# Six stacked cross layers on one core: a new order for all three engines in the steady unit, and one multiply done in two halves

## Chip, cores, metric

One core of a Trainium2 chip runs the whole program. The metric is device time in microseconds (us), as the median of a kernel's runs. Engines: PE does the matmuls, ACT empties PSUM, DVE does the elementwise work in SBUF.

## The reference

```python
B, F, D, L = 16384, 100, 16, 6
Din = min(F * D, 1024)                       # 1024
x = x0                                       # [16384, 1024] bf16
for l in range(6):
    proj = jnp.einsum('bd,de->be', x, ws[l]) + bs[l]
    x = x0 * proj + x
```

## The kernel before

Batch rows come in 16 pairs of 2 x 512. A **unit** is one pair in one layer, so there are 96 units. A unit computes `x W` by a Strassen-like scheme: seven block products P1 to P7, of which 5 and 2 are split once more into seven half-size inner products (`5p1` to `5p7`, `2p1` to `2p7`). The six units of the first pair and the last unit use a single level. The other 89 are the **steady units** that this text is about.

Names: `P6.0` is product 6, output column block 0 (four matmuls of 512 columns). `5p3` is an inner product (four matmuls of 256 columns). ACT: `E…` adds the bias while emptying a bank, `F.m`, `5f1`, `2f2` … copy one PSUM bank into another so that the next product can add to it, `5e_…` and `2e_…` empty inner results. DVE: `T1` to `T4` and `5t…`, `2t…` are the sums that feed products; `Q1, Ua, Va` finish blocks; `Qm, Um, Vm, Wm` multiply a block by x0; `Qa, Ux, Vx, Wx` add the old x, which completes the next unit's input. W is block 21.

```python
# cut: a rank per operation; one list for every steady unit (SPAN2 = 23.4 apart)
R2 = ranks("""
P1.0@0 5p1@.9 5p5@1.3 P1.1@1.7 P1.2@2.6 5p2@3.5 5p6@3.9 2p1@4.3 2p5@4.8 P1.3@5.2 5p3@6.1 5p7@6.5 2p2@7 2p6@7.4
5p4@8 P6.1@8.5 2p7@9.4 P6.0@9.8 ...
... E4.0@22.1 E4.3@22.7 E4.2@23.2 E4.1@23.8
T1@-1.1 5t13@.2 5t2@2.1 ... Va@21.4 Wm@24.6 Wx@26 Vm@27.9 Vx@29.4
""")
...
        for m in range(KH):      # the last product, and its evictions into W
            group(f"P4.{m}", "4", pA[m], A[m], T[4], ["T4", A[m]], m, False)
            biased(f"E4.{m}", W[:, m, :], pA[m][:], 1, m, [A[m]], [f"W.{m}"])
...
        for nm, C, q in (("Q", Q, (0, 0)), ("U", U, (0, 1)), ("V", V, (1, 1)), ("W", W, (1, 0))):
            ttop(nm + "m", C[:], C[:], blk(x0T, *q), MULT, allm(nm) + [X0[q]], allm(nm))
...
    # cut: operations are emitted greedily by rank once those they depend on are emitted
    heap = [(ops[i][0], i) for i in range(len(ops)) if need[i] == 0]
```

The ranks fix the order of the instructions on each engine. DVE and ACT then run their lists strictly in order (the Trainium skill says so, "Perfetto Trace Analysis", section Tensor Engine Instruction).

Of the kernel before, what the change touches and what calls it, by code (L numbers as in the profile page):

```python
# [10 lines left out]
MULT = mybir.AluOpType.mult  # L11
# [5 lines left out]
def ranks(text):  # L17

    return {w.split("@")[0]: float(w.split("@")[1]) for w in text.split()}
# [3 lines left out]


R2 = ranks("""
P1.0@0 5p1@.9 5p5@1.3 P1.1@1.7 P1.2@2.6 5p2@3.5 5p6@3.9 2p1@4.3 2p5@4.8 P1.3@5.2 5p3@6.1 5p7@6.5 2p2@7 2p6@7.4
5p4@8 P6.1@8.5 2p7@9.4 P6.0@9.8 P3.1@10.7 2p3@11.5 2p4@12 P3.0@12.4 P6.3@13.3 P6.2@14.1 P3.3@15 P3.2@15.9
P7.3@16.7 P7.0@17.6 P7.2@18.4 P7.1@19.3 P4.3@20.2 P4.0@21 P4.2@21.9 P4.1@22.8
5e_p5@2 5f1@2.6 E1.1@3.1 E1.2@3.7 5e_c11@4.2 E1.0@4.7 5f2@5.3 2e_p5@5.7 2f1@6.4 5e_c12@6.8 5e_u3@7.3 2e_c11@7.8
2f2@8.4 E1.3@8.9 F.1@9.6 5e_c21@10 2e_u3@10.5 F.0@11 2e_c12@12.2 E3.1@12.7 2e_c21@13.2 E3.0@13.7 F.3@14.3  # L30
F.2@15.2 E3.3@16.1 E3.2@16.9 E7.3@17.8 E7.2@19.5 E7.0@20.1 E7.1@20.7 E4.0@22.1 E4.3@22.7 E4.2@23.2 E4.1@23.8
T1@-1.1 5t13@.2 5t2@2.1 2t13@3.7 5t4@5.4 2t2@6.9 T2@7.2 T4@8.5 T3@9.6 2t4@10.8 5cc@11.1 2cc@12.8 Q1@13.9 Qm@15.1
Qa@16.4 Ua@17.6 Um@18.9 Ux@20.2 Va@21.4 Wm@24.6 Wx@26 Vm@27.9 Vx@29.4
""")
R0 = ranks("""
P1.0@0 P1.1@.9 P1.2@1.7 P1.3@2.6 P2.2@3.5 P2.3@4.4 P2.1@5.2 P2.0@6.1 P5.2@6.9 P5.1@7.8 P5.0@8.7 P5.3@9.5
# [2 lines left out]
F1.2@2.8 F1.0@3.2 F1.3@3.7 F1.1@4.1 E2.2@4.6 E2.1@6.3 E2.0@7.2 E2.3@7.7 E5.2@8.3 F.2@11.5 E5.1@11.9 E5.3@12.4  # L39
F.1@13.2 E5.0@13.6 E7.2@14.9 E3.2@15.8 F.0@16.4 E7.1@16.8 F.3@17.4 E3.1@17.8 E7.0@19.2 E3.0@19.8 E3.3@20.4  # L40
E7.3@21 E4.0@21.8 E4.2@22.7 E4.1@23.6 E4.3@24.4
Qm@14.5 Qa@18.6 Ua@21.1 Um@22.4 Va@23.5 Wm@25.2 Wx@26.4 Ux@27.6 T1@4.6 Vm@30 Vx@31.2 T2@8.3 T3@9.8 T4@13
c5@-8.6 c6@-6.8 c7@-4.5 c3@11.9 2i7@-7.4 2i5@-7.1 2i6@.5 2i3@9.4 5i5@10.9 5i7@11.2 5i6@11.6 5i3@14.2
""")
RFIRST = {**R0, **ranks("""
# [6 lines left out]
def kernel(  # L52
# [18 lines left out]
    KQ, HQ, NQ = KH // 2, H // 2, NB // 2  # L71
# [20 lines left out]
    P1s, P5s, Q, U, V, W = (work.tile([P, KH, NB], BF16, name=f"ev{i}") for i in range(6))  # L92
# [6 lines left out]
    def blk(t, dh, n):  # L99
        return t[:, n, dh * KH:(dh + 1) * KH, :]  # L100

    def tt(o, a, b, op):
        nc.vector.tensor_tensor(out=o, in0=a, in1=b, op=op)  # L103
# [60 lines left out]
    def op(rank, fn, rd=(), wr=(), weights=()):  # L164
        for k in weights:
            uses_left[k] = uses_left.get(k, 0) + 1
        ops.append((rank, fn, tuple(rd), tuple(wr), tuple(weights)))
# [3 lines left out]
    for u, (pr, l) in enumerate(units):  # L171
        one, first, last = level1(u), u == 0, u == NU - 1
        rk = RFIRST if first else (R0 if one else R2)
        x0T, xst = x0Ts[pr % 2], xsts[pr % 2]
        xs = x0T if l == 0 else xst
        X0 = {q: f"x0.{pr % 2}.{q[0]}{q[1]}" for q in QD}
# [3 lines left out]
        def add(name, fn, rd=(), wr=(), weights=(), rk=rk, base=base, u=u):  # L180
            op(base + rk[name], fn, rd, wr, [(u, w) for w in weights])

        def ttop(name, o, a, b, o_, rd, wr, **kw):
            add(name, lambda: tt(o, a, b, o_), rd, wr, **kw)
# [64 lines left out]
        if not one:  # L249
            for X, Bm, src in (("5", T[1][:], "T1"), ("2", B21, XI[1, 0])):  # L250
                q = lambda dh, n, Bm=Bm: Bm[:, dh * KQ:(dh + 1) * KQ, n * NQ:(n + 1) * NQ]
# [15 lines left out]
        if not one:  # L267
            for X, Bm, src, a, b, C in (("5", T[1][:], "T1", 0, 1, P5s), ("2", B21, XI[1, 0], 2, 3, Q)):
                q = lambda dh, n, Bm=Bm: Bm[:, dh * KQ:(dh + 1) * KQ, n * NQ:(n + 1) * NQ]
# [49 lines left out]
        allm = lambda s: [f"{s}.{m}" for m in range(KH)]  # L319
# [2 lines left out]
        ttop("Ua", U[:], U[:], P5s[:], ADD, allm("U") + allm("5c"), allm("U"))  # L322
        ttop("Va", V[:], V[:], P5s[:], ADD, allm("V") + allm("5c"), allm("V"))
        for nm, C, q in (("Q", Q, (0, 0)), ("U", U, (0, 1)), ("V", V, (1, 1)), ("W", W, (1, 0))):
            ttop(nm + "m", C[:], C[:], blk(x0T, *q), MULT, allm(nm) + [X0[q]], allm(nm))
            if not last:
                ttop(nm + ("a" if nm == "Q" else "x"), blk(xst, *q), C[:], blk(xs, *q), ADD, allm(nm) + [XI[q]], [XO[q]])
            else:
                xfin = xsts[1 - pr % 2][:].rearrange("r n k (j p) -> r (n k j) p", p=P).rearrange(
                    "r (e n j k) p -> r e n j k p", e=2, n=2, j=KH)  # L330
                xo = x0Ts[1 - pr % 2][:].rearrange("r n k (j p) -> r (n k j) p", p=P).rearrange(
                    "r (e n j k) p -> r e n j k p", e=2, n=2, j=KH)
                XF = [f"xs.{1 - pr % 2}.{a}{b}" for a, b in QD]
                XT = [f"x0.{1 - pr % 2}.{a}{b}" for a, b in QD]
                eh, n = q

                def fin(eh=eh, n=n, C=C, xfin=xfin, xs=xs):
                    v4 = lambda a: a.rearrange("r k (j p) -> r k j p", p=P)
                    tt(xfin[:, eh, n].rearrange("r j k p -> r k j p"), v4(C[:]), v4(blk(xs, eh, n)), ADD)
                add(nm + ("a" if nm == "Q" else "x"), fin, allm(nm) + [XI[q]] + XF, [f"xf{eh}{n}"])  # L340

                def tr(eh=eh, n=n, xfin=xfin, xo=xo):
                    nc.sync.dma_start_transpose(out=xo[:, eh, n].rearrange("p j k r -> p (j k) r"),
                                                in_=xfin[:, eh, n].rearrange("r j k p -> r (j k p)"))
                z = base + {"Q": 40, "U": 41, "V": 42, "W": 43}[nm]
                op(z, tr, [f"xf{eh}{n}"] + XT, [f"xt{eh}{n}"])

                def st(eh=eh, n=n, xo=xo, pr=pr):
                    r0 = pr * PR + n * NB
                    nc.sync.dma_start(out[r0:r0 + NB, eh * H:(eh + 1) * H].rearrange("(j p) d -> p j d", p=P),  # L350
                                      xo[:, eh, n].rearrange("p j k r -> p j (k r)"))
                op(z + 10, st, [f"xt{eh}{n}"], ["out"])
# [110 lines left out]
```

## Time and profile before

| | before |
|---|---|
| time, median of 3 runs | 2318.92 us (2318.32 to 2319.11) |
| PE / DVE / ACT busy | 98% / 91% / 79% |
| a steady unit, start to start | 23.63 us, in layer 1 (counted from 0) 23.68; the 88 after the first average 23.65 |
| the same at the pitch of undelayed groups (20 of 0.863 us, 14 of 0.437) | 23.38 us |

From the page of the kernel before: the span, the busy times, and the first line of the chain that ended last.

```profile
span 2316.6 us, 34627 instructions
...
PE 2272.3 (98%) x12674; PEld 1261.3 (54%) x12912; DVE 2102.9 (91%) x2218; ACT 1837.5 (79%) x3223; POOL 20.4 (1%) x41
...
PE 95%; DVE 2%; issue 1%; DMA 1%; SPq 0%; ACT 0%; DVEq 0%; ACTq 0%
```

PE is the bound, but "98% busy" hides the question. The ends of matmuls are modelled, so small gaps vanish in it (a group of four is drawn 1.03 us long below and repeats every 0.86), and one has to read **start to start**. Here is one steady unit, from the timeline of PE of the kernel before. The columns are start in us, length in us, engine, line, operation, out<-in, shapes, count; neighbours that look alike are merged. This trace misses some matmul records (12674 of 12912 are there), so a group of four can show as x3.

```profile
1088.91 1.03 PE L189 MATMUL pA<-xst,wp 128*128 128x512 bf16 x4
1089.77 0.60 PE L287 MATMUL pX<-T,wp 128*128 128x256 bf16 x4
...
1095.42 0.60 PE L287 MATMUL pX<-ti,wp 128*128 128x256 bf16 x4
1095.98 0.60 PE L287 MATMUL pX<-xst,wp 128*128 128x256 bf16 x4
1096.41 1.16 PE L287 MATMUL pX<-ti,wp 128*128 128x256 bf16 x8
1097.41 1.03 PE L189 MATMUL pA<-T,wp 128*128 128x512 bf16 x4
...
1105.63 7.07 PE L189 MATMUL pA<-T,wp 128*128 128x512 bf16 x32
1112.54 1.03 PE L189 MATMUL pA<-xst,wp 128*128 128x512 bf16 x3
```

P1.0 and the group after it start 0.86 us apart; 2p2 and 2p6 (1095.98, 1096.41) 0.43 us. P7 and P4 at 1105.63 take 6.91 us for 32 matmuls, 216 ns each. Against that, 5p7 at 1095.42 is followed by 2p2 after 0.56 us, 0.12 too many. 2p6 and 5p4 (x8 at 1096.41) take 1.00 us where two groups need 0.87, another 0.13 (0.12 in the unrounded starts). From 1088.91 to 1112.54 it is 23.63 us.

ACT at that place, in the kernel before:

```profile
1095.36 0.57 ACT L194 COPY pX<-pX 128x512 f32<-128x512 f32 x1
1095.84 1.08 ACT L194 CAST iu<-pX 128x512 bf16<-128x512 f32 x2
```

The copy is 2f1. It ends at 1095.93, and 2p2, which adds to that bank, starts at 1095.98. The second of the two casts, 5e_u3, empties the bank that 5p4 needs: it ends at 1095.84 + 1.08 = 1096.92, and 5p4 starts 0.44 us before P6.1, at 1096.97. So ACT holds both. DVE in the same unit (T1, 5t13, Wm, 5t2, Wx, 2t13, and after the cut T2 with T4):

```profile
1087.81 1.22 DVE L103 TENSOR_TENSOR T<-xst 128x2048 bf16<-128x2048 bf16 x1
1089.13 0.69 DVE L103 TENSOR_TENSOR ti<-T 128x1024 bf16<-128x1024 bf16 x1
1089.84 1.22 DVE L103 TENSOR_TENSOR ev<-ev,x0T 128x2048 bf16<-128x2048 bf16 x1
1090.98 0.42 DVE L103 TENSOR_TENSOR ti<-T,ti 128x512 bf16<-128x512 bf16 x1
1091.31 1.22 DVE L103 TENSOR_TENSOR xst<-ev,xst 128x2048 bf16<-128x2048 bf16 x1
1092.57 0.69 DVE L103 TENSOR_TENSOR ti<-xst 128x1024 bf16<-128x1024 bf16 x1
...
1096.12 2.54 DVE L103 TENSOR_TENSOR T<-xst,T 128x2048 bf16<-128x2048 bf16 x2
```

T1 to 5t13, which reads what T1 just wrote, is 1.32 us; Wm to 5t2, which are independent, is 1.14. T2 ends at 1096.12 + 1.22 = 1097.34, and P6.1, its first reader, starts at 1097.41. DVE is therefore **just in time** as well.

The duration of 1.22 us is the one that the Trainium skill gives for this operation ("VectorE: DVE Perf Modes", the perf-mode tier table: 1224 ns for a bf16 tensor_tensor of 2048 columns).

### The profile page before, as it was taken

The numbers are of one execution on the slowest core, as the hardware profiler recorded it, in microseconds if no ns is written. First come the engines' busy times: TensorE is split into PE (matmuls) and PEld (weight loads), VectorE is DVE, ScalarE is ACT, GpSimd is POOL, SyncE is SP. The second block draws the span as 40 slices with busy tenths as digits, with TensorE's granted clock in tenths as the row PEclk, the third lists the DMA queues.
The fourth block names the chain that finished last, engine by engine and source line by source line (L and its number), as shares of the span: only waits on it lengthen the run. The fifth ranks groups of instructions, "written<-read, shape, count | busy, mean of one in ns | idle before, by whom it ended". The sixth has DMA issues, their size and how long they took to land.

```text
span 2316.6 us, 34627 instructions
## 1 busy us (share of the span) xinstructions
PE 2272.3 (98%) x12674; PEld 1261.3 (54%) x12912; DVE 2102.9 (91%) x2218; ACT 1837.5 (79%) x3223; POOL 20.4 (1%) x41
## 2 busy tenths in 40 slices
PE   8999999999999999999999999999999999999996
PEld 3445555555555555555555555555555555555552
DVE  6999999999999999999999999999999999999995
ACT  4768887888888887888788887878888888878884
POOL 1100000000000000000000000000000000000000
PEclk9999999999999999999999999999999999999998
DMA  9679588695977969779696795968869697795953
GB/s 300 237 239 312 193 242 275 195 315 191 243 263 212 301 209 250 254 225 282 212 281 231 219 286 196 295 216 236 278 193 294 207 251 265 205 313 192 272 183 73
DMA packets 627931, 558.05 MB, mean 241 GB/s; under 512 B 401712, under 2 KB 554288, under 8 KB 627760
## 3 DMA queue, kind: packets, MB, share of 16 engines
q1 hardware_dynamic: 622576, 536.95, 76.9%
q0 software_dynamic: 5184, 18.88, 2.0%
q8 instruction: 101, 1.65, 0.3%
q14 instruction: 70, 0.57, 0.1%
HBM read 436.21 MB, written 52.43 MB: 211 GB/s over the span
## 4 chain that ended last, share of the span: by engine, by line
PE 95%; DVE 2%; issue 1%; DMA 1%; SPq 0%; ACT 0%; DVEq 0%; ACTq 0%
PE pA L189 55%; PE pX L287 24%; PE pX L189 16%; DVE ev L103 1%; DVE xst L103 1%; SPq L384 0%; DVE T L103 0%; DMA Lc<-isum 0%; DMA x0T<-in_x_dram 0%; DVE wp L103 0%; ACT ev L198 0%; DVE ti L103 0%; SPq L391 0%; DVE isum L103 0%; ACT pX L194 0%
## 5 line engine op out<-in xcount | busy, mean ns | idle before, releaser
L189 PEld LDWEIGHTS <-wp 128*128 128x128 bf16 x7904 | 772.1, 98 | 853.3 <-issue 12.2
L189 PE MATMUL pA<-T,wp 128*128 128x512 bf16 x4512 | 1051.8, 379 | 5.5 <-DVE T L103 0.4
L198 ACT ACTIVATE ev<-pA,b_all 128x512 bf16<-128x512 f32 x1124 | 720.0, 688 | 187.9 <-PE pA L189 187.9
L287 PEld LDWEIGHTS <-wp 128*128 128x128 bf16 x4984 | 486.4, 98 | 175.7 <-issue 1.9
L103 DVE TENSOR_TENSOR ev<-ev,x0T 128x2048 bf16<-128x2048 bf16 x384 | 469.7, 1223 | 9.9 <-ACT ev L198 2.3
L287 PE MATMUL pX<-ti,wp 128*128 128x256 bf16 x2848 | 423.1, 272 | 1.6 <-DVE ti L103 1.6
L103 DVE TENSOR_TENSOR xst<-ev,xst 128x2048 bf16<-128x2048 bf16 x320 | 390.5, 1222 | 11.6
L103 DVE TENSOR_TENSOR ev<-ev,ev 128x2048 bf16<-128x2048 bf16 x281 | 344.2, 1225 | 47.7 <-ACT ev L194 33.1
L189 PE MATMUL pX<-xst,wp 128*128 128x512 bf16 x1328 | 334.5, 378 | 4.9 <-DVE xst L103 2.2
L198 ACT ACTIVATE ev<-pX,b_all 128x512 bf16<-128x512 f32 x412 | 284.1, 694 | 54.8 <-PE pX L189 46.7
L189 PE MATMUL pA<-xst,wp 128*128 128x512 bf16 x1203 | 302.2, 379 | 4.0
L194 ACT COPY pX<-pA 128x512 f32<-128x512 f32 x412 | 239.9, 587 | 69.5 <-PE pA L189 66.7
L194 ACT CAST iu<-pX 128x512 bf16<-128x512 f32 x356 | 202.0, 596 | 43.4 <-PE pX L287 43.3
L194 ACT CAST ev<-pX 128x512 bf16<-128x512 f32 x384 | 227.5, 595 | 0.3 <-PE pX L189 0.2
L194 ACT COPY pX<-pX 128x512 f32<-128x512 f32 x356 | 206.2, 579 | 8.5
L103 DVE TENSOR_TENSOR T<-xst,T 128x2048 bf16<-128x2048 bf16 x160 | 195.5, 1222 | 8.0
L103 DVE TENSOR_TENSOR ev<-iu,ip 128x1024 bf16<-128x1024 bf16 x178 | 122.5, 688 | 85.9 <-ACT iu L194 85.9
L103 DVE TENSOR_TENSOR T<-xst 128x2048 bf16<-128x2048 bf16 x160 | 195.0, 1219 | 0.5
L194 ACT CAST ip<-pX 128x512 bf16<-128x512 f32 x178 | 106.1, 596 | 94.2 <-PE pX L287 94.2
L287 PE MATMUL pX<-T,wp 128*128 128x256 bf16 x1068 | 160.2, 273 | 0.1
L287 PE MATMUL pX<-xst,wp 128*128 128x256 bf16 x888 | 133.0, 272 | 0.0
L103 DVE TENSOR_TENSOR xst<-ev,x0T 128x2048 bf16<-128x2048 bf16 x64 | 78.1, 1222 | 1.1
(30 smaller groups left out, 614.8 us busy)
## 6 DMA issues: line engine op xcount, KB each, us to landing
wp<-Lc SPq DMA_DIRECT2D x538, 512.0 KB, 4.4
wp<-in_ws_dram SPq DMA_DIRECT2D x288, 512.0 KB, 5.3
out_dram<-x0T SPq DMA_DIRECT2D x30, 1024.0 KB, 9.9
Lc<-wp POOLq DMA_DIRECT2D x24, 512.0 KB, 6.0
Lc<-isum POOLq DMA_DIRECT2D x12, 512.0 KB, 3.7
w<-in_ws_dram SPq DMA_DIRECT2D x6, 512.0 KB, 7.6
out_dram<-x0T SPq DMA_DIRECT2D x4, 512.0 KB, 4.7
x0T<-in_x_dram SPq DMA_TRANSPOSE x34, 7.3
```

The lines of the kernel that those rows point to most:

```text
L103: nc.vector.tensor_tensor(out=o, in0=a, in1=b, op=op)
L189: nc.tensor.matmul(bank[:], lhsT=wt[(u, w)][:, k, m * P:(m + 1) * P], rhs=rhs[:, k, :], start=(start and k == 0), stop=(k == KH - 1), skip ...
L194: add(name, lambda: nc.scalar.copy(out=dst, in_=src), rd, wr)
L198: add(name, lambda: nc.scalar.activation(out=dst, in_=src, func=IDENT, bias=b_all[:, c:c + 1], scale=1.0), rd, wr)
L287: nc.tensor.matmul(pX[bank][:, m * NQ:(m + 1) * NQ], lhsT=wv[:, k, m * P:(m + 1) * P], rhs=rhs[:, k, :], start=(start and m == 0 and k == ...
```

## The change

Its intent is to remove the two gaps before 2p2 and 5p4 by a new order of products and evictions, with a DVE order to match. The multiply of W by x0 is cut in two so that its first half can run before all of W is there.

```diff
 R2 = ranks("""                                   # cut to the entries used below
-P1.0@0 5p1@.9 5p5@1.3 P1.1@1.7 P1.2@2.6 5p2@3.5 5p6@3.9 2p1@4.3 2p5@4.8 P1.3@5.2 5p3@6.1 5p7@6.5 2p2@7 2p6@7.4
-5p4@8 P6.1@8.5 2p7@9.4 P6.0@9.8 P3.1@10.7 2p3@11.5 2p4@12 P3.0@12.4 ...
+P1.0@0 P1.2@0.86 5p5@1.73 5p1@2.16 P1.3@2.6 2p1@3.46 5p2@3.9 5p6@4.34 2p5@4.78 P1.1@5.21 5p7@6.08 5p3@6.51 2p2@6.95
+2p6@7.39 5p4@7.82 P6.0@8.26 P6.1@9.13 2p7@9.99 2p3@10.43 P3.0@10.86 2p4@11.73 P6.2@12.16 ...
-... 2f1@6.4 5e_c12@6.8 5e_u3@7.3 2e_c11@7.8 2f2@8.4 E1.3@8.9 ... E4.0@22.1 E4.3@22.7 E4.2@23.2 E4.1@23.8
+... 2f1@6.3 5e_u3@6.75 E1.3@7.23 E1.1@7.8 2e_c11@8.37 5e_c21@8.85 2f2@9.33 F.0@9.78 5e_c12@10.23 ... E4.0@21.87 E4.1@22.44 E4.2@23.01 E4.3@23.59
-T1@-1.1 5t13@.2 5t2@2.1 2t13@3.7 5t4@5.4 2t2@6.9 T2@7.2 T4@8.5 T3@9.6 2t4@10.8 5cc@11.1 2cc@12.8 ... Va@21.4 Wm@24.6 Wx@26 Vm@27.9 Vx@29.4
+T1@-1.14 5t13@0.59 5t2@3.06 2t13@3.39 5t4@5.13 2t2@6.6 T2@6.93 2t4@8.07 T4@8.4 5cc@10.88 T3@11.48 2cc@12.61 ... Va@21.11 Wma@23.38 Wmb@24.58 Wx@25.31 Vm@27.38 Vx@28.85
 """)
@@ R0, the single-level units
-... Wm@25.2 ...
+... Wma@25.2 Wmb@25.3 ...
@@
         for nm, C, q in (("Q", Q, (0, 0)), ("U", U, (0, 1)), ("V", V, (1, 1)), ("W", W, (1, 0))):
-            ttop(nm + "m", C[:], C[:], blk(x0T, *q), MULT, allm(nm) + [X0[q]], allm(nm))
+            if nm == "W":
+                for h, g in enumerate("ab"):
+                    sl, ms = slice(h * KQ, (h + 1) * KQ), [f"W.{2 * h}", f"W.{2 * h + 1}"]
+                    ttop("Wm" + g, C[:, sl], C[:, sl], blk(x0T, *q)[:, sl], MULT, ms + [X0[q]], ms)
+            else:
+                ttop(nm + "m", C[:], C[:], blk(x0T, *q), MULT, allm(nm) + [X0[q]], allm(nm))
```

On DVE the order T1, 5t13, Wm, 5t2, Wx becomes T1, **Wma**, 5t13, **Wmb**, Wx, 5t2.

More of the change, by code (lines that the diff above doesn't have):

```diff
@@ L25 @@
 R2 = ranks("""
-P1.0@0 5p1@.9 5p5@1.3 P1.1@1.7 P1.2@2.6 5p2@3.5 5p6@3.9 2p1@4.3 2p5@4.8 P1.3@5.2 5p3@6.1 5p7@6.5 2p2@7 2p6@7.4
-5p4@8 P6.1@8.5 2p7@9.4 P6.0@9.8 P3.1@10.7 2p3@11.5 2p4@12 P3.0@12.4 P6.3@13.3 P6.2@14.1 P3.3@15 P3.2@15.9
-P7.3@16.7 P7.0@17.6 P7.2@18.4 P7.1@19.3 P4.3@20.2 P4.0@21 P4.2@21.9 P4.1@22.8
-5e_p5@2 5f1@2.6 E1.1@3.1 E1.2@3.7 5e_c11@4.2 E1.0@4.7 5f2@5.3 2e_p5@5.7 2f1@6.4 5e_c12@6.8 5e_u3@7.3 2e_c11@7.8
-2f2@8.4 E1.3@8.9 F.1@9.6 5e_c21@10 2e_u3@10.5 F.0@11 2e_c12@12.2 E3.1@12.7 2e_c21@13.2 E3.0@13.7 F.3@14.3
-F.2@15.2 E3.3@16.1 E3.2@16.9 E7.3@17.8 E7.2@19.5 E7.0@20.1 E7.1@20.7 E4.0@22.1 E4.3@22.7 E4.2@23.2 E4.1@23.8
-T1@-1.1 5t13@.2 5t2@2.1 2t13@3.7 5t4@5.4 2t2@6.9 T2@7.2 T4@8.5 T3@9.6 2t4@10.8 5cc@11.1 2cc@12.8 Q1@13.9 Qm@15.1
-Qa@16.4 Ua@17.6 Um@18.9 Ux@20.2 Va@21.4 Wm@24.6 Wx@26 Vm@27.9 Vx@29.4
+P1.0@0 P1.2@0.86 5p5@1.73 5p1@2.16 P1.3@2.6 2p1@3.46 5p2@3.9 5p6@4.34 2p5@4.78 P1.1@5.21 5p7@6.08 5p3@6.51 2p2@6.95
+2p6@7.39 5p4@7.82 P6.0@8.26 P6.1@9.13 2p7@9.99 2p3@10.43 P3.0@10.86 2p4@11.73 P6.2@12.16 P3.1@13.03 P6.3@13.89
+P3.2@14.75 P3.3@15.62 P7.1@16.48 P7.0@17.34 P7.2@18.21 P7.3@19.07 P4.1@19.93 P4.0@20.8 P4.2@21.66 P4.3@22.52
+E1.0@1.07 5e_p5@2.38 5f1@3.03 E1.2@3.48 5e_c11@4.55 5f2@5.2 2e_p5@5.65 2f1@6.3 5e_u3@6.75 E1.3@7.23 E1.1@7.8
+2e_c11@8.37 5e_c21@8.85 2f2@9.33 F.0@9.78 5e_c12@10.23 2e_u3@10.71 2e_c12@11.18 F.1@11.66 E3.0@12.11 2e_c21@12.68
+F.2@13.23 E3.1@14.1 F.3@14.96 E3.2@15.82 E3.3@16.69 E7.0@18.41 E7.1@18.98 E7.2@19.55 E7.3@20.14 E4.0@21.87 E4.1@22.44
+E4.2@23.01 E4.3@23.59
+T1@-1.14 5t13@0.59 5t2@3.06 2t13@3.39 5t4@5.13 2t2@6.6 T2@6.93 2t4@8.07 T4@8.4 5cc@10.88 T3@11.48 2cc@12.61 Q1@13.35
+Qm@14.62 Qa@15.89 Ua@17.43 Um@18.7 Ux@19.97 Va@21.11 Wma@23.38 Wmb@24.58 Wx@25.31 Vm@27.38 Vx@28.85
 """)
@@ L41 @@
 E7.3@21 E4.0@21.8 E4.2@22.7 E4.1@23.6 E4.3@24.4
-Qm@14.5 Qa@18.6 Ua@21.1 Um@22.4 Va@23.5 Wm@25.2 Wx@26.4 Ux@27.6 T1@4.6 Vm@30 Vx@31.2 T2@8.3 T3@9.8 T4@13
+Qm@14.5 Qa@18.6 Ua@21.1 Um@22.4 Va@23.5 Wma@25.2 Wmb@25.3 Wx@26.4 Ux@27.6 T1@4.6 Vm@30 Vx@31.2 T2@8.3 T3@9.8 T4@13
 c5@-8.6 c6@-6.8 c7@-4.5 c3@11.9 2i7@-7.4 2i5@-7.1 2i6@.5 2i3@9.4 5i5@10.9 5i7@11.2 5i6@11.6 5i3@14.2
```

## The prediction

> **What bounds the kernel now.** The matmul stream: the busy line has PE at 98%, the chain of waits puts 95% of the span on it; DVE is busy 91%, ACT 79%. PE busy says little about headroom (Trainium skill, "Perfetto Trace Analysis", Identifying the Most-Contended Engine), so I read start to start. In the PE timeline a steady unit (89 of 96) takes 23.63 us, sometimes 23.68; mean over the steady stretch 23.68 (2107.24 us / 89). Undelayed groups repeat every 0.864 us (four 512-column matmuls, 216 ns each) and 0.438 us (four 256-column, 109 ns), which agrees with the Trainium skill, "TensorE: Matmul & The Clock Gate", Back-to-back issue gap: N/2.4 + 2.5 ns. A steady unit has 20 and 14 groups: 20 x 0.864 + 14 x 0.438 = 23.41 us. So 0.22 to 0.27 us a unit is stall, about 24 us in all, 1%. It lies at two places: before 2p2 (0.12 us; ACT copies its bank at 1024.42 for 0.57 us, 2p2 starts 1025.04) and before 5p4 (0.12 us, behind the ACT cast 5e_u3). DVE is just in time too (T2 ends 1097.34, its first reader starts 1097.41), so it would hold P6 even if ACT did not.
>
> **What the change does.** No matmul, ACT operation or DMA byte is added or removed. Products and evictions are interleaved so that each ACT copy comes earlier than the matmul that needs its bank. On DVE one 2048-column multiply (1.22 us; 1.14 start to start) becomes two of 1024 columns (0.69; 0.60): +0.06 us, 96 times. DVE has some 1.8 us idle a unit, so this by itself costs nothing. The first half waits only for W's first two evictions (the build has thresholds two evictions apart), so it fills the slot between T1 and 5t13, where DVE loses about 0.2 us now; 2t13 no longer stands right behind Wx.
>
> **Slack at the matmul floor, estimated from measured latencies** (matmul group start to ACT start 1.07 or 0.64 us; ACT copy start to matmul 0.62; ACT pitch 0.48 copy, 0.58 activation, 0.64 dependent copy). 2p2 wanted at 6.95 us after P1.0, ready 6.92; 2p7 9.99, ready 9.95 to 10.0; P3.3 15.62, ready 15.58; 2p6 has 0.3. DVE: from Ua (starts 17.43, after E3.3) to T2 is one busy chain of 12.9 to 13.0 us; P6.0, wanted at 8.26, is ready 8.25 to 8.31. Both old stalls go, and several edges keep under 0.05 us. I expect 23.43 to 23.47 us a unit, not 23.41.
>
> **Time.** 88 regular units x (23.67 - 23.45) = 19 us saved. The first pair and the last unit keep their order; there the split adds under 1 us. The first steady unit (25.86 us, waits for ti) changes by under 1 us. Predicted 2299.5 us, 0.8% less; range 2295 to 2312. Faster by over 2%: 0.01; within 2%: 0.98; slower by over 2%: 0.01. Saving 2% would need 46 us, twice all the stalls.
>
> **What would show it.** Right: PE repeats at about 23.45; no gap before 2p2 or 5p4; DVE's wait before 5cc stays over 1 us; granted clock still 0.995. Wrong: a repeating gap before P6.0 (DVE chain), before 2p2, 2p7, P3.1 or P3.3 (ACT), or before 5p5 (5t13).
>
> **What would make it wrong.** A tight edge missing by 0.1 us in every unit costs 9 us; two of them eat the gain. Five irregular units (23.82 to 23.91 us now) may grow, since DVE runs longer without idle before P6.0. Late weight loads are unlikely: tiles come free within about 1 us of the old order.

## The result, and the profile after

| | before | after |
|---|---|---|
| time, median of 4 runs each | 2318.74 us (2318.32 to 2319.11) | 2299.23 us (2298.99 to 2301.13) |
| ratio, 95% interval | | 0.9918 (0.9901 to 0.9935) |
| span of the profiled run, granted clock | 2316.6 us, 0.995 | 2297.4 us, 0.995 |
| mean of the 88 steady units after the first | 23.65 us | 23.45 us |
| units over 23.75 us among those 88 | 5 | 0 |

A ratio is the mean time of one kernel's fast runs over the mean of the other's fast runs of the same rounds, so it is not quite the ratio of the medians.

Where the 19.2 us of span came from, by unit starts on PE: the 88 steady units gave 18.0 us (2081.38 - 2063.41), the first steady unit 0.95 (25.86 - 24.91), the last unit with the tail 0.5 (45.08 - 44.57). The start up to the first steady unit lost 0.2 (164.28 to 164.51), which is within what this start varies from run to run (163.95 to 166.88 us in the traces below).

From the page of the changed kernel:

```profile
span 2297.4 us, 34637 instructions
...
PE 2255.7 (98%) x12674; PEld 1261.1 (55%) x12912; DVE 2079.1 (90%) x2314; ACT 1833.8 (80%) x3223; POOL 20.3 (1%) x41
...
PE 96%; DVE 2%; issue 1%; DMA 1%; SPq 1%; ACT 0%; DVEq 0%; ACTq 0%
```

By these lines almost nothing happened: PE is at 98% in both, and DVE executes 96 instructions more. The difference is in the starts. Timeline of PE of the changed kernel, the steady unit that begins at 1080.49:

```profile
1087.44 0.60 PE L288 MATMUL pX<-xst,wp 128*128 128x256 bf16 x4
1087.88 1.04 PE L288 MATMUL pX<-ti,wp 128*128 128x256 bf16 x8
1088.75 1.89 PE L190 MATMUL pA<-T,wp 128*128 128x512 bf16 x8
1090.54 0.60 PE L288 MATMUL pX<-ti,wp 128*128 128x256 bf16 x4
...
1103.94 1.24 PE L190 MATMUL pA<-xst,wp 128*128 128x512 bf16 x4
```

2p2 (1087.44) to 2p6 is 0.44, and 2p6 with 5p4 take 0.87: both old gaps are gone. P6.0 and P6.1 (x8 at 1088.75) need 1.73, and 2p7 starts after 1.79. That is the one gap left, 0.06 us. The unit takes 1103.94 - 1080.49 = 23.45 us. ACT of the changed kernel there (2f1, then further on 2f2):

```profile
1086.80 0.57 ACT L195 COPY pX<-pX 128x512 f32<-128x512 f32 x1
...
1089.85 0.64 ACT L195 COPY pX<-pX 128x512 f32<-128x512 f32 x1
```

2f1 ends at 1087.37 for 2p2 at 1087.44. 2f2 ends at 1090.49, and 2p7, which needs its bank, starts 0.05 us later. DVE of the changed kernel (T1, Wma, 5t13, Wmb, Wx, and after the cut T2):

```profile
1079.30 1.22 DVE L104 TENSOR_TENSOR T<-xst 128x2048 bf16<-128x2048 bf16 x1
1080.44 0.69 DVE L104 TENSOR_TENSOR ev<-ev,x0T 128x1024 bf16<-128x1024 bf16 x1
1081.04 0.68 DVE L104 TENSOR_TENSOR ti<-T 128x1024 bf16<-128x1024 bf16 x1
1081.64 0.69 DVE L104 TENSOR_TENSOR ev<-ev,x0T 128x1024 bf16<-128x1024 bf16 x1
1082.43 1.23 DVE L104 TENSOR_TENSOR xst<-ev,xst 128x2048 bf16<-128x2048 bf16 x1
...
1087.45 1.22 DVE L104 TENSOR_TENSOR T<-xst,T 128x2048 bf16<-128x2048 bf16 x1
```

The starts are 1.14, 0.60, 0.60 and 0.79 us apart, with no idle time that the profile marks; the 0.79 is before Wx, which reads what Wmb has just written. T1 to T2 is 8.15 us, where it was 8.31. T2 ends at 1088.67, and P6.0 starts 0.08 us later. Where P6.0 really waits for T2 it starts 0.05 to 0.06 us after T2's end (`unsplit_late`, `pad_chain` below), so the slack is 0.02 to 0.03 us (0.09 in the units of layer 1).

### The profile page after: what moved, and what is told of

Read it like the earlier page. It is cut to its first block, busy times and chain, and to the rows that moved or that the text cites. A ratio compares the mean times of both kernels' runs of the same rounds, so it can differ in the third digit from the quotient of the medians.

```text
span 2297.4 us, 34637 instructions
## 1 busy us (share of the span) xinstructions
PE 2255.7 (98%) x12674; PEld 1261.1 (55%) x12912; DVE 2079.1 (90%) x2314; ACT 1833.8 (80%) x3223; POOL 20.3 (1%) x41
## 4 chain that ended last, share of the span: by engine, by line
PE 96%; DVE 2%; issue 1%; DMA 1%; SPq 1%; ACT 0%; DVEq 0%; ACTq 0%
PE pA L190 56%; PE pX L288 24%; PE pX L190 16%; DVE ev L104 1%; SPq L390 0%; DMA Lc<-isum 0%; DMA x0T<-in_x_dram 0%; DVE xst L104 0%; DVE wp L104 0%; DVE T L104 0%; ACT ev L199 0%; DVE isum L104 0%; SPq L397 0%; ACT pX L195 0%; DVE ti L104 0%
## 5 line engine op out<-in xcount | busy, mean ns | idle before, releaser
L199 ACT ACTIVATE ev<-pA,b_all 128x512 bf16<-128x512 f32 x1124 | 706.0, 689 | 212.8 <-PE pA L190 166.0
L104 DVE TENSOR_TENSOR ev<-ev,x0T 128x2048 bf16<-128x2048 bf16 (+1 forms) x480 | 482.8, 1007 | 7.7 <-ACT ev L199 1.3
L104 DVE TENSOR_TENSOR xst<-ev,xst 128x2048 bf16<-128x2048 bf16 x320 | 391.1, 1224 | 19.4 <-DVE ev L104 0.5
L288 PE MATMUL pX<-ti,wp 128*128 128x256 bf16 x2848 | 398.1, 272 | 0.6 <-DVE ti L104 0.6
L199 ACT ACTIVATE ev<-pX,b_all 128x512 bf16<-128x512 f32 x412 | 288.9, 705 | 65.2 <-PE pX L190 46.8
L195 ACT COPY pX<-pA 128x512 f32<-128x512 f32 x412 | 256.3, 627 | 63.5 <-PE pA L190 60.8
L104 DVE TENSOR_TENSOR ev<-iu,ip 128x1024 bf16<-128x1024 bf16 x178 | 122.5, 688 | 121.1 <-ACT iu L195 121.1
L195 ACT CAST iu<-pX 128x512 bf16<-128x512 f32 x356 | 196.8, 639 | 0.3 <-PE pX L288 0.2
```

The source lines that it names most:

```text
L104: nc.vector.tensor_tensor(out=o, in0=a, in1=b, op=op)
L195: add(name, lambda: nc.scalar.copy(out=dst, in_=src), rd, wr)
L199: add(name, lambda: nc.scalar.activation(out=dst, in_=src, func=IDENT, bias=b_all[:, c:c + 1], scale=1.0), rd, wr)
L288: nc.tensor.matmul(pX[bank][:, m * NQ:(m + 1) * NQ], lhsT=wv[:, k, m * P:(m + 1) * P], rhs=rhs[:, k, :], start=(start and m == 0 and k == ...
```

## The experiments

Three theories stood at the start. **A:** in the kernel before, ACT's bank copies and the DVE chain up to T2 both hold the matmuls, so neither half of the change pays without the other. **B:** it was ACT alone. **C:** the DVE order with the split is what pays. Ten kernels were run; all results are correct. They ran: the first four kernels and the next four on one chip, the last two on another. "Unit" is the mean of the 88 steady units after the first, from the trace.

| kernel | median us | ratio to before | unit us |
|---|---|---|---|
| `split_alone` | 2322.18 | 1.0017 (1.0002 to 1.0031) | 23.70 |
| `dve_only` | 2316.73 | 0.9992 (0.9978 to 1.0007) | 23.64 |
| `pe_act_only` | 2317.00 | 0.9996 (0.9979 to 1.0013) | 23.63 |
| `unsplit_late` | 2320.23 | 1.0007 (0.9992 to 1.0022) | 23.67 |
| `again` (the changed kernel) | 2299.34 | 0.9917 (0.9903 to 0.9930) | 23.45 |
| `e13_late` | 2295.77 | 0.9899 (0.9885 to 0.9912) | 23.40 |
| `pad_chain` | 2321.21 | 1.0008 (0.9995 to 1.0022) | 23.69 |
| `pad_idle` | 2299.32 | 0.9913 (0.9900 to 0.9927) | 23.45 |
| `swap_halves` | 2378.76 | 1.0259 (1.0242 to 1.0276) | 24.34 |
| `unsplit_early` | 2395.08 | 1.0329 (1.0313 to 1.0344) | 24.53 |

The kernel before: 2318.58, 2318.79 and 2318.96 us.

### `split_alone`: the old order, only the multiply cut

```diff
 # the changed kernel's code with the ranks of before
-Wm@24.6
+Wma@24.6 Wmb@24.61
```

> The kernel before, with W's multiply in two adjacent halves and no operation moved. Theory A (before, both ACT's bank copies and the DVE chain that ends in T2 hold the matmuls; both had to go): the split adds about 0.06 us to the DVE chain up to T2, which has 0.02 us of slack, so a steady unit takes 23.67 to 23.70 us and the kernel 2319 to 2323 us; units of the first pair shorten from 24.34 to about 24.30, as they did in the changed kernel. Theory B (ACT's bank copies alone): 2318 to 2319, steady unit 23.63 unchanged. Theory C (the DVE order and the split alone make the gain): towards 2310 or less.

Measured: 2322.18 us, 3.6 us slower than before; most units take 23.68. In the first pair a unit takes 24.30, as it does in the changed kernel, where before it took 24.34. So the halves by themselves cost a little. In the trace of `split_alone` T1 to T2 has grown by 0.07 us, and P6.1 starts 0.05 us after T2's end in every layer but layer 0; in the kernel before, only layer 1 did so regularly. The 0.06 us that they add to the DVE chain is not absorbed by DVE's idle time elsewhere, because T2 was already just in time. C's short form (the split pays by itself) is out.

### `dve_only`: the new DVE order, the old PE and ACT order

```diff
 # the changed kernel, but P1..P3, P6, inner products and their evictions with the ranks of before
-P1.0@0 P1.2@0.86 5p5@1.73 5p1@2.16 ... 2f1@6.3 5e_u3@6.75 E1.3@7.23 ...
+P1.0@0 5p1@.9 5p5@1.3 P1.1@1.7 ... 2f1@6.4 ... 5e_u3@7.3 ...
 # kept from the change: P7, P4, E7, E4 and every DVE rank
```

> The new DVE order with the split; PE and ACT in the old order, except that the last two products and their evictions stand in the new order, so that the first half finds its data early. Theories A and B: the gaps before 2p2 and 5p4 stay, 0.12 us each, a steady unit 23.60 to 23.65, 2312 to 2319 us. Theory C: 23.45 a unit, about 2299 us.

Measured: 2316.73 us, 86 of 88 units at 23.63 or 23.64. PE timeline of `dve_only` (5p7, 2p2, then 2p6 with 5p4, then P6.1):

```profile
1141.91 0.60 PE L286 MATMUL pX<-ti,wp 128*128 128x256 bf16 x4
1142.47 0.60 PE L286 MATMUL pX<-xst,wp 128*128 128x256 bf16 x4
1142.90 1.16 PE L286 MATMUL pX<-ti,wp 128*128 128x256 bf16 x8
1143.90 1.03 PE L188 MATMUL pA<-T,wp 128*128 128x512 bf16 x4
```

5p7 to 2p2 is 0.56, and 2p6 with 5p4 take 1.00: the same two gaps, although T2 now ends 0.32 us before P6.1 starts. So they are not DVE's. What the new DVE order did remove is the occasional 23.68, three of the five long units (there are two left) and 0.94 us of the first steady unit (24.92), together some 2 us.

### `pe_act_only`: the new PE and ACT order, DVE as before

```diff
 # the code of before, with the changed kernel's P, E, F and inner ranks; all DVE ranks of before
-T1@-1.14 5t13@0.59 ... Wma@23.38 Wmb@24.58 Wx@25.31 ...
+T1@-1.1 5t13@.2 5t2@2.1 ... Wm@24.6 Wx@26 ...
```

> The new order of PE and ACT; DVE exactly as in the kernel before, no split. Theory A: the chain on DVE from Va to T2 takes 9.45 us and not 9.21; 0.10 us of that is slack, so P6.0 starts about 0.14 us late in each unit, 23.52 to 23.60 us a unit, 2306 to 2313 us. Theory B: 23.45, 2299 us. Theory C: about 2318 us.

Measured: 2317.00 us, where A expected 2306 to 2313. The two old gaps are gone and the time stays, because new gaps take their place, the main one at another edge than A had named. First the PE timeline (P1.3, then 2p1), then from DVE's the Wx of the same unit:

```profile
1138.13 1.03 PE L188 MATMUL pA<-xst,wp 128*128 128x512 bf16 x4
1139.20 0.60 PE L286 MATMUL pX<-xst,wp 128*128 128x256 bf16 x4
```

```profile
1137.93 1.22 DVE L102 TENSOR_TENSOR xst<-ev,xst 128x2048 bf16<-128x2048 bf16 x1
```

2p1 reads block 21 of x, which Wx writes. The new PE order asks for it 3.46 us after P1.0 and not at 4.3. With the old DVE order Wx ends at 1139.15, and 2p1 starts at 1139.20, 0.21 us late. Of this, 0.17 us is idle time of DVE before the whole multiply Wm, which waits for the last eviction of W, E4.3. The cross-check is in the units of layer 0: their 2p1 reads x0, not Wx's result, and every sixth period is 23.48 or 23.49 us, while nearly all others take 23.65 to 23.68. In these units the edge that A had named does show: P6.0 starts 0.10 us late, 0.05 us after T2's end (A had expected 0.14).

So A stands in its main statement and B and C fall: each half alone gave 1.6 to 1.9 us, which the intervals of their ratios do not tell from nothing, and both together 19.5. But A's arithmetic had overlooked an edge.

### `unsplit_late`: the changed kernel, multiply whole

```diff
 # the code of before with all new ranks; the whole multiply in the second half's place
-Wma@23.38 Wmb@24.58
+Wm@24.58
```

> The changed kernel with W's multiply whole, in the place of its second half (after 5t13). Theory A from the measured pitches: T1 to Wx start 3.19 us and not 3.06 (1.33 + 0.60 + 1.26 against 1.14 + 0.60 + 0.60 + 0.72), so T2 is 0.13 us later, of which 0.10 is slack and 0.05 hides behind the gap before 2p7: 23.44 to 23.48 us a unit, 2299 to 2303 us; the split is worth at most 3 us. The rival (the split is what makes the gain): 2308 us or more.

Measured: 2320.23 us, 23.68 a unit. The expectation drawn from A (2299 to 2303) was plainly wrong: with the multiply whole in this place, the new order gains nothing. DVE timeline of `unsplit_late` (T1, 5t13, Wm, Wx); the bracket is the idle time before an operation and who ended it:

```profile
1137.16 1.22 DVE L102 TENSOR_TENSOR T<-xst 128x2048 bf16<-128x2048 bf16 x1
1138.42 0.69 DVE L102 TENSOR_TENSOR ti<-T 128x1024 bf16<-128x1024 bf16 x1
1139.28 1.23 DVE L102 TENSOR_TENSOR ev<-ev,x0T 128x2048 bf16<-128x2048 bf16 x1 [0.17 <-ACT ev L197]
1140.61 1.23 DVE L102 TENSOR_TENSOR xst<-ev,xst 128x2048 bf16<-128x2048 bf16 x1
```

I had put 0.60 us between 5t13 and Wm, the pitch of a 1024-column operation. It is 0.86, since the whole multiply waits for E4.3, the last eviction of the unit. T1 to Wx is 3.45 us, where the changed kernel needs 3.13 (1082.43 - 1079.30, a unit of layer 3; this one is of layer 5, where it is the same). In this unit 2p1 is 0.07 late and P6.0 a further 0.22.

In the kernel before the same wait was all but hidden. Its last eviction of W ends about 0.9 us after P1.0 too (in one unit ACT ends at 1066.17, P1.0 started at 1065.28), but its T1 and 5t13 stood about 0.1 us later against P1.0 (T1 1.10 us ahead of it and not 1.20), so Wm followed 5t13 after 0.71 us with no idle time that the profile marks.

### `swap_halves`: is it the size, or what the first half waits for?

```diff
-                for h, g in enumerate("ab"):
+                for h, g in ((1, "a"), (0, "b")):
```

> The changed kernel with the two halves of W's multiply exchanged: the same two operations of the same size in the same two slots, but the one between T1 and 5t13 now takes the columns of evictions E4.2 and E4.3, the last of the unit. If the split pays because its first half waits for E4.0 and E4.1 alone: E4.3 ends about 0.95 us after T1's successor could start, 5t13 comes about 0.95 us late, 5p5 follows about 0.5 us late and 2p1 and P6.0 behind the later Wx and T2, 0.5 to 0.95 us a unit, 2340 to 2385 us. If it pays because of its size, or because a slot between dependent operations is filled: 2299 us.

The two operations and their places are the same; only the columns are exchanged. Measured: 2378.76 us, 24.34 a unit. DVE timeline of `swap_halves` (T1, the first half, 5t13):

```profile
1137.64 1.22 DVE L104 TENSOR_TENSOR T<-xst 128x2048 bf16<-128x2048 bf16 x1
1139.76 0.69 DVE L104 TENSOR_TENSOR ev<-ev,x0T 128x1024 bf16<-128x1024 bf16 x1 [0.90 <-ACT ev L199]
1140.37 0.69 DVE L104 TENSOR_TENSOR ti<-T 128x1024 bf16<-128x1024 bf16 x1
```

DVE stands still for 0.90 us waiting for ACT, although 5t13 behind it had its data: the queue is strictly in order. So the half pays by **which evictions it waits for**: two halves of the same size in the same places, with the late evictions first, are 2.6% slower than the kernel before.

### `unsplit_early`: the whole multiply in the first half's place

```diff
-Wma@23.38 Wmb@24.58
+Wm@23.38
```

> The changed kernel with W's multiply whole in the place of its first half. It waits for E4.3 as in the exchange of the halves, and 5t13 stands behind 1.14 us of multiply and not 0.60: about 1.0 us late for 5p5, 24.3 to 24.5 us a unit, 2375 to 2392 us, clearly slower than the whole multiply after 5t13 (23.68 a unit, 2320 us). If the wait plays no part: within 0.1 us a unit of that.

Measured: 2395.08 us, 24.53 a unit, somewhat beyond the range. The DVE wait before the multiply is again 0.90 us. PE of `unsplit_early` (P1.0 with P1.2, then 5p5):

```profile
1170.49 1.89 PE L188 MATMUL pA<-xst,wp 128*128 128x512 bf16 x8
1173.30 0.60 PE L286 MATMUL pX<-ti,wp 128*128 128x256 bf16 x4 [0.92 <-DVE ti L102]
```

By starts, 5p5 is 2.81 - 1.73 = 1.08 us late; the bracket says 0.92 because it counts from the modelled end of the matmul before. Most of the loss is the wait for E4.3, which `swap_halves` has too; that the multiply is whole costs another 0.19 us a unit (24.53 against 24.34).

### `pad_chain` and `pad_idle`: where does DVE have slack?

```diff
+    scr = const.tile([P, NB], BF16, name="scr")
...
         if not one:
+            ttop("pad", scr[:], zeros[:], zeros[:], ADD, [], ["scr"])
 # pad_chain: rank 5.5, between Vx and 2t2;   pad_idle: rank 9.0, between T4 and 5cc
```

> The changed kernel with one more DVE operation of 512 columns a unit (0.33 us pitch, result unused) between Vx and 2t2, inside the chain to T2. Theory A: P6.0 starts 0.33 - 0.10 us late, 23.60 to 23.65 us a unit, 2312 to 2318 us. Rival (DVE is 90% busy with over 1.3 us idle a unit, so 0.33 us more is free): 2299 us.

> The same extra operation between T4 and 5cc, where DVE waits 1.4 us. Every theory: 2299 us, 23.45 us a unit, DVE's wait before 5cc down from 1.4 to about 1.05 us.

Measured: 0.33 us of DVE work in the chain costs 21.9 us (2321.21 against 2299.34 of `again`, 0.24 us a unit); the same work before 5cc costs nothing (2299.32). In the trace DVE's wait for the data of 5cc falls from 1.38 us (121.1 us over 88 waits) to 1.04 (91.4 over 88). `pad_chain` lies above its range. I had taken the slack of T2 as 0.10 us from a single unit of layer 1; in the others it is about 0.03. PE of `pad_chain` (2p6 with 5p4, then P6.0), then its T2 from DVE:

```profile
1144.46 1.03 PE L287 MATMUL pX<-ti,wp 128*128 128x256 bf16 x8
1145.60 1.89 PE L189 MATMUL pA<-T,wp 128*128 128x512 bf16 x8
```

```profile
1144.32 1.22 DVE L103 TENSOR_TENSOR T<-xst,T 128x2048 bf16<-128x2048 bf16 x1
```

T2 ends at 1145.54 and P6.0 starts 0.06 us later. It is 0.27 us behind its place at 1144.46 + 0.87; 0.33 less a slack of 0.03 gives 0.30, and it is made up of this and 0.04 before 2p6. The unit grows by 0.24 only, since the gap of 0.06 before 2p7 no longer shows.

### `again` and `e13_late`: the gap that is left

```diff
-5e_u3@6.75 E1.3@7.23 E1.1@7.8 2e_c11@8.37 5e_c21@8.85 2f2@9.33 F.0@9.78
+5e_u3@6.75 E1.1@7.23 2e_c11@7.8 2f2@8.44 5e_c21@8.92 E1.3@9.4 F.0@9.78
```

> The changed kernel once more, as a yardstick on this chip: 2299 us, 23.45 us a steady unit, one gap of 0.05 us a unit left, before 2p7.

> The changed kernel, with ACT's eviction E1.3 (not needed until P6.3) moved behind the bank copy 2f2 and 2f2 ahead of 5e_c21, nothing else. If the 0.05 us before 2p7 is the wait for 2f2 and nothing else is as tight: 2f2 starts some 0.9 us earlier, the gap goes, 23.39 to 23.41 us a unit, 2294 to 2297 us. Rival: another edge (T2 to P6.0 has 0.10 us) takes over at once: 2298 to 2300 us.

E1.3 empties a bank that nobody needs before P6.3, but it stood ahead of 2f2, which PE waits for. The run also moves 2f2 ahead of 5e_c21, and the two moves were not tried apart. Measured: 2295.77 us (2294.91 to 2297.11) beside 2299.34 of `again` on the same chip (2298.57 to 2301.06; no run of one lies within the range of the other), 23.38 to 23.40 us in 86 of 88 units. The intervals of the two ratios to before overlap slightly; the traces agree with the medians, 0.05 us x 88 = 4.4 us. PE of `e13_late` (P6.0 with P6.1, then 2p7), then its 2f2 from ACT:

```profile
1042.67 1.89 PE L188 MATMUL pA<-T,wp 128*128 128x512 bf16 x8
1044.40 0.60 PE L286 MATMUL pX<-ti,wp 128*128 128x256 bf16 x4
```

```profile
1042.89 0.57 ACT L193 COPY pX<-pX 128x512 f32<-128x512 f32 x1
```

2p7 follows after 1.73 us, and 2f2 ends 0.94 us before it. The undelayed groups sum to 20 x 0.863 + 14 x 0.437 = 23.38 us; what the starts still show is 0.01 us before P3.3. This is the best kernel, 1.0% under before.

## Why the prediction was right, point by point

- **Time.** Predicted 2299.5 us, range 2295 to 2312; measured 2299.23. A unit: predicted 23.43 to 23.47, measured 23.45. The first steady unit: under 1 us, measured 0.95. That the total hits within 0.3 us is partly luck: the prediction took 19.4 us from the 88 units, counting 23.67 us each where they averaged 23.65, and they gave 18.0; the first steady unit and the last one gave 1.45 (0.95 and 0.5), for which it had booked no gain.
- **The stalls.** The two gaps before 2p2 and 5p4 were the right ones for ACT (`dve_only` keeps them and keeps the time). "It would hold P6 even if ACT did not" is right for the kernel before: `split_alone` adds 0.06 us to that chain and the units get longer. Under the new PE order with the old DVE order, however, the edge that held most units was Wx to 2p1 (`pe_act_only`), which the prediction did not list; T2 to P6.0 held the units of layer 0. The new DVE order meets it, with 1083.95 - 1083.66 = 0.29 us from Wx's end to 2p1 in the unit shown.
- **The slack list.** 2p7 "ready 9.95 to 10.0" was the gap that appeared, 0.05 us a unit. P6.0 "ready 8.25 to 8.31" came out at 8.23 to 8.24 (T2's end at 1088.67 and 0.05 to 0.06 us), so P6.0 started at 8.26 without a wait. P3.3, also on the list, is 0.01 us late.
- **What the split is for.** The prediction named the right condition (only the first two evictions) and gave as its worth some 0.2 us of lost pitch. The runs show a larger worth: without the split this order is at 23.67 (`unsplit_late`), and with the halves exchanged at 24.34 (`swap_halves`). The term that I had missed is the wait for E4.3.
- **"This by itself costs nothing"** was wrong as a statement about the split: alone it cost 3.6 us (`split_alone`). Idle time later in the unit does not pay for work in a chain without slack.
- **The irregular units** did not grow but went from five to none over 23.75 us. The trace shows where the five lose their time: in three, one DVE operation (5t13 once, Wx twice) starts 0.20 to 0.35 us later than in other units, and 2p6 and P6.1 follow late; in two, the ACT copy F.2 starts 0.28 us late, and P3.2 with it. What delays these operations stays open. In the changed kernel one unit shows the same on a small scale (Qa 0.35 us late, 23.54 us), and longer ones still occur singly in other kernels (two of 23.91 in `pad_chain`, one of 23.76 in `e13_late`).

## What to carry to other kernels

When the bounding engine is 98% busy, sum the undelayed pitch of its work and compare it with the period; the difference is the whole prize, here 0.27 us in 23.65. Follow every tight edge by start times on all engines, for removing the gap of one engine is worth nothing while another's chain is just in time behind it: each half of this change alone gave under 2 us, both together 19.5. Split an operation where its first part can start on data that is ready earlier, and check which producers each part waits for; on an engine that runs in order, the same split with the halves exchanged cost 79 us (2378.76 against 2299.34).

## What the Trainium skill lacked or had wrong

- "TensorE: Matmul & The Clock Gate", Back-to-back issue gap: N/2.4 + 2.5 ns, which the page gives for an isolated matmul, holds in the stream here: 216 ns at 512 columns (6.91 us for 32 matmuls) and 109 ns at 256 (0.437 us for 4), with a weight load before every matmul. The same section's figure of about 131 ns per 512-column matmul in a stream of weight loads and matmuls does not appear in any of these traces, where no 512-column matmul is followed within less than 214 ns.
- "VectorE: DVE Perf Modes", The DRAIN you can't avoid, says of copies that a semaphore between operations costs nothing extra. Here a 2048-column tensor_tensor is followed after 1.14 us by an independent one and after 1.25 to 1.33 us by one that reads its result; the trace does not tell how much of that is the semaphore.
- "Perfetto Trace Analysis" warns that matmul busy time is a poor measure and offers utilization (MFU) and weight-load busy time in its place. In these runs PE busy was 98% in both kernels and weight loads 54% and 55%, which cannot show a gap of 0.05 us either; start-to-start periods did.
- No page was found that gives the delay from one engine's result to another's start. In these traces a matmul group starts 0.05 to 0.06 us after the recorded end of the ACT copy or DVE operation that it waits for.
